# A recurrent-memory transformer layer: a new order of TensorE work, wider last-row projection, kept weights, no padding loads

## The chip, the cores and the metric

The kernel runs on one core of a Trainium2 chip. The metric is device time in microseconds (us), from one launch to its end; lower is better. "PE" is TensorE (its matmuls), "PEld" its weight loads, "DVE" VectorE, "ACT" ScalarE, "POOL" GpSimd and "SP" SyncE, whose queue issues the DMAs.

## The reference, cut to what matters

```python
# x (1, 2048, 512), mem0 (1, 8, 512), 32 heads of 128, seg_len 32, bf16
h  = x + A(layernorm(x))
h2 = h + B(layernorm(h))

def A(x):
    mem = mem0
    for s in range(64):
        xs = x[:, 32 * s:32 * s + 32]
        hcat = concat([mem, xs])                # 8 memory rows + 32 token rows
        q, k, v = (einsum('btd,dhe->bhte', hcat, W) for W in (Wq, Wk, Wv))
        scores = einsum('bhqe,bhke->bhqk', q, k) * 128 ** -0.5
        scores = where(mask, scores, -1e9)      # memory seen by all; tokens causal
        o = einsum('bhqk,bhke->bhqe', softmax(scores), v)
        o = einsum('bhte,hed->btd', o, Wo)
        mem = o[:, :8]                          # feeds the next segment
        outs.append(o[:, 8:])
    return concat(outs)

def B(x):                                       # MLP, inner width 1792
    return einsum('bsf,fd->bsd', gelu(einsum('bsd,df->bsf', x, w1) + b1), w2) + b2
```

The memory rows that a segment puts out are the memory rows that the next one takes in, so the 64 segments run one after the other. The MLP is free of that chain.

## The kernel before, in words

**Rows.** A segment has 8 memory rows and 32 token rows. The kernel works on packs of 32 rows: pack A of a segment holds its first 24 token rows (`NA`) and the 8 memory rows. The last 8 token rows of four segments make pack B of a block of 128 tokens (`hB`, `KB`, `QTB`, `VSB`, `VBD`, `OTB`). Pack B depends on no memory, so its Q, K and V are computed a block ahead. `bk = s // 4` is the block of segment `s` and `sg = s % 4` its place in it.

**Work of one segment on PE.** Each name below is a stage in the tuple `ORDER`, which fixes by hand the order of PE's work in a segment, in units (stage, from unit, to unit).

- `Q0 K0 Q1 K1 V0 V1`: projections of pack A, half of the heads each. A pass (`passes`, L670) is four units, one for each 128 of the contraction of 512; a unit is four matmuls 512 wide on the four 32-column tiles of the array, each with its weight load of 128x32 (`hT`). ACT casts the result out of PSUM into `kq` (L688, L689), DVE transposes it (L711) into `KALL` and `QT`; `ZC` (L725, L732) takes the memory and last-row queries.
- `SC0 SC1` (`sc_mm`, L815): scores of the memory rows and last rows, 16 heads each; then `sc_softmax`: maximum `nmc`, exponential `EC`, reciprocal `rsc`, product `PC`, transpose `PTC` (L824 to L835). A score bank is filled with the mask ahead of the matmuls (`prefill`).
- `SA` (`sa_mm`, L874): scores of the 24 token rows, and the softmax into `PTA`.
- `PV0 PV1` (`pv_c`, L846 and L850): value products of memory and last rows, with the array tiled by rows; copies to `OT` and `OTB`.
- `PVA` (`pv_a`, L903): value products of the token rows of the segment before, also tiled by rows; `pv_a_ev` copies them to `OT`.
- `WO` (`wo`, `wo_units`, L931): output projection, 64 matmuls 256 wide in 8 units; its 32 rows are this segment's memory rows and the token rows of an earlier segment. DVE transposes the result (`TT`, L943) and adds its two halves (L937): the memory columns of the next segment's `hT`, and the token rows into `opT`.
- `F0 F1`: in `sg` 0, 1 and 2 the K, Q and V passes of the next block's pack B; in `sg` 3 the output projection of pack B of the block before (`wo_B`), in eight units that take the place of the passes.

**Out of the recurrence.** `nat` brings `opT` by a DMA transpose into `oN`, adds it to the residual `xr` (L967), takes the statistics for the second layer norm and writes `h_mid`. It runs two blocks behind. The MLP runs at the end, in four superblocks of 512 tokens (L1260, L1267, L1313); some of its loads and first matmuls lie in the last segments.

**Order on the other engines.** `Sched` records every operation with what it reads and writes. PE's order is as written; DVE, ACT, POOL and SP get theirs from list scheduling with estimated durations, in which `BONUS` shifts priorities by kind. An operation with alternatives (`either`) goes to ACT or DVE. `BANK` says which PSUM bank each stage uses: 0 to 3 are `quad`, 4 to 7 `ps`.

**Alignment.** `align` counts PE instructions and, with `PHASE` set, puts up to eight padding weight loads into a pass (L668) until every segment starts at a chosen count modulo 256. With `KEEP` set, the passes run through the contraction forth and back (`directions`), and a unit whose weights are those already loaded is issued as `matmul_kept`, without loads.

The order of one segment before:

```python
ORDER = (("PVA", 0, 99), ("Q0", 0, 4), ("K0", 0, 4), ("Q1", 0, 4), ("K1", 0, 4), ("SC0", 0, 99), ("V0", 0, 4),
         ("V1", 0, 2), ("SC1", 0, 99), ("SA", 0, 99), ("V1", 2, 4), ("F0", 0, 2), ("PV0", 0, 99), ("F0", 2, 4),
         ("PV1", 0, 99), ("WO", 0, 8), ("F1", 0, 4))
```

Of the kernel before, what the change touches and what calls it, by code (L numbers as in the profile page):

```python
# [27 lines left out]
BONUS = {"EC0": 9.64, "EC1": 2.52, "KA1": 1.19, "KB0": -4.21, "KB1": 40, "OTB": -3, "OTm0": 25.44, "OTm1": -8.14, "OTx": 40, "PA": -3.16, "PC0": 2.46, "PC1":  # L28
# [3 lines left out]
         4.71, "kq1": 12.67, "kq2": 10.08, "kq5": 6.67, "maskA": -7.3, "maskAF": -11.82, "maskCF": -12.78, "maskL": 40, "maskR": 2.12, "nma": -4.99,  # L32
         "nmc0": 40, "nmc1": 40, "oN": -40, "opA": 4.9, "opB": -1.91, "rs": 40, "rs2": -8.34, "rsa": -1.22, "rsc0": -3.89, "rsc1": -3.1, "sma": -4.13,
         "st2": -40, "vd": -1.71, "xT": 0.29, "xn": -10, "xr": 3.08}
LEAN = 0.36
# [13 lines left out]
class Op:  # L49
    __slots__ = ("eng", "fn", "reads", "writes", "idx", "gidx", "deps", "sig", "sigcount", "waits",  # L50
                 "tag", "pad", "held", "name", "is_dma", "dma_sem", "dur", "mode", "rank", "start", "succ", "prev", "ni", "dma_count", "alts", "kind")

    def __init__(self, eng, fn, reads, writes, name, dur, mode):
        self.eng, self.fn, self.reads, self.writes = eng, fn, reads, writes
        self.name, self.dur, self.mode = name, dur, mode
        self.deps, self.waits, self.succ = [], [], []
        self.tag = self.pad = self.held = None
        self.sig = self.is_dma = False
        self.sigcount = 0
        self.dma_sem = None  # L60
        self.rank = self.start = 0.0
        self.idx = -1
        self.prev = None
        self.alts = None
        k = writes[0] if writes else ""
        self.kind = k if isinstance(k, str) else k[0] + (str(k[-1]) if k[0] in HALVES else "")


class Sched:
# [181 lines left out]
    def finalize(self):  # L251
# [5 lines left out]
        for o in self.all_ops:  # L257
            E = o.eng
            cand, dwaits = {}, []
            for p in o.deps:  # L260
                if p.is_dma:
                    if p not in dma_known[E]:
                        dwaits.append(p)
                    continue
                if p.eng == E and E not in self.self_sync:
                    continue
                if p.idx > cand.get(p.eng, -1):
                    cand[p.eng] = p.idx
            waits = []
            for F, i in cand.items():  # L270
# [107 lines left out]
P = 128  # L378
# [62 lines left out]
def build_kernel(nc, A_x, A_mem0, A_Wq, A_Wk, A_Wv, A_Wo, B_w1, B_b1, B_w2, B_b2, out):  # L441
# [3 lines left out]
    with st:  # L445
# [47 lines left out]
        TT = sb("TT", [P, 2, DC, 2, 32], F32)  # L493
        TTB = sb("TTB", [P, DC, 2, 32], F32)
        opT = sb("opT", [P, 2, DC, P])
# [342 lines left out]
        def pv_c(s, r):  # L838
            par, bk, sg = s % 2, s // 4, s % 4

            def f(e):
                for i in range(4):
                    for j in range(4):
                        rows = slice(32 * j, 32 * j + 32)
                        c0 = 16 * (i % 2)
                        e.matmul(quad[:, j, (4 * r + i) * 16:(4 * r + i) * 16 + 16], VS[rows, s % 3, r, i * E:(i + 1) * E], PTC[rows, r, c0:c0 + 16, i // 2],  # L846
                                 start=(i == 0), stop=False, tile_position=(32 * j, 0), skip_group_check=True)
                for j in range(4):
# [16 lines left out]
        def sa_mm(s, bank):  # L865
            par = s % 2

            prefill("maskAF", maskAF, 256, ps[bank][:, 0:256], ("ps", bank))

            def f(e):  # L870
                for k in range(8):
                    for j in range(4):
                        h = 16 * (k // 4) + 4 * j + k % 4
                        ins = e.matmul(ps[bank][32 * j:32 * j + 32, 32 * k:32 * k + 32], QT[:, h // 2, :, h % 2], KALL[:, par * HP + h // 2, :, h % 2], start=False, stop=(k == 7),  # L874
                                       tile_position=(0, 32 * j), skip_group_check=True)
                return ins
            S.op("pe", f, reads=[("QT", 0), ("QT", 1), ("KA", par, 0), ("KA", par, 1)], writes=[("ps", bank)], dur=0.25, mode=MC, ni=64)
            v = ps[bank][:, 0:256].rearrange("p (a t) -> p a t", a=8)

# [16 lines left out]
        def pv_a(s):  # L896
            par = s % 3

            def f(e):
                for k in range(8):  # L900
                    for j in range(4):
                        rows = slice(32 * j, 32 * j + 32)
                        ins = e.matmul(quad[:, j, 256 + 24 * k:280 + 24 * k], VS[rows, par, k // 4, (k % 4) * E:(k % 4 + 1) * E], PTA[rows, s % 2, k // 2, 0:NA, k % 2],  # L903
                                       start=(s == NS - 1 and k == 0), stop=True, tile_position=(32 * j, 0), skip_group_check=True)
                return ins
            S.op("pe", f, reads=[("VS", par, 0), ("VS", par, 1), ("PTA", s % 2)], writes=QK, dur=0.26, mode=MR, ni=64)

        def pv_a_ev(s):
            opar = s % 2
            src = quad[:, :, 256:448].rearrange("p j (k q) -> p j k q", k=8)  # L910
            ot = OT[:, opar, :, 0:NA].rearrange("p (j k) q -> p j k q", k=8)
# [42 lines left out]
        def wo_B(bk, bank):  # L954
            wo_units(lambda sl: OTB[:, bk % 2, sl, :], lambda r: [("OTB", bk % 2, sg) for sg in range(4)], bank)
            S.op("dve", lambda e: e.transpose(TTB[:].rearrange("p c q t -> p (c q t)"), ps[bank][:, 0:256]), reads=[("ps", bank)], writes=["TTB"], dur=t_dve(256) + 0.02)
            t5 = TTB[:].rearrange("p c q (s t) -> p c q s t", s=4)
            o = opT[:, bk % 2, :, :].rearrange("p c (s t) -> p c s t", s=4)[:, :, :, NA:SEG]
            S.op("dve", lambda e: [e.tensor_tensor(o[64 * q2:64 * q2 + 64], t5[0:64, :, q2], t5[64:128, :, q2], ALU.add) for q2 in range(2)][1],
                 reads=["TTB"], writes=[("opB", bk % 2)], dur=0.6)  # L960

        def nat(bk):

            S.dma(lambda e: e.dma_start_transpose(oN[:], opT[:, bk % 2].rearrange("p c t -> p (c t)")), 256,
                  reads=[("opA", bk % 2, k) for k in range(4)] + [("opB", bk % 2)], writes=["oN"])
            xs = xr[:, bk % XR, :]
            S.op("dve", lambda e: e.tensor_tensor(xs, xs, oN[:].rearrange("p c t -> p (c t)"), ALU.add), reads=["oN", ("xr", bk % XR)], writes=[("xr", bk % XR)], dur=0.43)  # L967
            i = bk % 2
# [122 lines left out]
        for s in range(NS):  # L1091
# [46 lines left out]
            def after_pv1(f):  # L1138
                if "PV1" in done or not any(n[:2] == "SC" for n in done):
                    f()  # L1140
# [5 lines left out]
            def part(name):  # L1146
# [46 lines left out]
                elif name == "SA":  # L1193
                    sa_mm(s, bank_of[name])
                elif name == "PVA":
                    if s > 0:
# [9 lines left out]
            if s == 0:  # L1206

                for n in START:
# [15 lines left out]
                    elif n == "X":  # L1224
                        ln1(1)
                    elif n == "Z":
                        qb_fill(0)
# [53 lines left out]
        for i in range(2):  # L1281
# [3 lines left out]
        p2_T(1)  # L1285

        rest = [lambda: wo(NS, 6, mem=False), lambda: pv_a(NS - 1), lambda: pv_a_ev(NS - 1), lambda: nat(NTB - 2), lambda: wo(NS + 1, 7, mem=False),
                lambda: wo_B(NTB - 1, 6), lambda: None, lambda: nat(NTB - 1)]
# [83 lines left out]
```

## Time and profile before

| | |
|---|---|
| runs | 861.02 us median of 3 (857.36 to 864.41) |
| profiled execution | span 869.8 us |
| PE | 92% busy, 22,121 matmuls |
| PEld | 57% busy, 24,182 weight loads |
| DVE | 66%, 1,870 instructions |
| ACT | 64%, 1,547 instructions |
| POOL | 10%, 205 instructions |
| mean granted clock | 0.986 |
| segments 1 to 62 | 57.00 to 750.66 us |
| before and after them | 57.00 us and 119.14 us |

The profiled execution is 8.8 us longer than the median of the runs. Its first 57 us are the loading of the weights and segment 0. Then follow 62 segments of the same shape, and at the end the last segment and the MLP. Nearly all the time lies in the 62 segments, so the thing to read is one segment, instruction by instruction. In a timeline, a group's length runs to the end of its last instruction while the next group has already begun; the time it takes from PE is the distance to the next group's start.

### The profile page before, as it was taken

The page shows a single profiled execution, that of the slowest core. Times are in us where ns is not written, and L with a number is a line of the kernel's source. Part 1 is how long each engine was busy: PE and PEld are TensorE (multiplying, and loading weights), DVE is VectorE, ACT ScalarE, POOL GpSimd, SP SyncE. Part 2 cuts the span into 40 slices and gives each one's busy share as a digit, 9 for nine tenths or more (in the row PEclk, how much of TensorE's full clock was granted, in tenths as well). Part 3 has the DMA queues.
Part 4 walks back from the last instruction along what each step waited for, and adds up shares of the span by engine and source line. Part 5 has one row for each costly group of instructions (what it writes and reads, how often), then busy time and mean ns, then how long its engine had stood idle before and what let it go on. Part 6 is the DMA issues. An engine that isn't in the chain of part 4 may idle for free.

```text
span 869.8 us, 50658 instructions
## 1 busy us (share of the span) xinstructions
PE 800.3 (92%) x22121; PEld 492.4 (57%) x24182; DVE 576.8 (66%) x1870; ACT 555.6 (64%) x1547; POOL 87.5 (10%) x205
## 2 busy tenths in 40 slices
PE   3588999999999999999999998999999999889998
PEld 1245666666656666666656665665656665544443
DVE  3267677878787878787878786867687867534111
ACT  2347676767676767676767776767676758922332
POOL 4021000101010101010010101000000000006200
PEclk9879999999999999999999999999999999999999
DMA  9951000110101010101010101010113120254100
GB/s 357 366 163 22 5 26 19 28 30 25 31 23 34 23 35 19 32 20 37 16 40 16 41 17 40 11 34 11 34 28 65 46 77 16 87 171 112 49 24 25
DMA packets 65937, 49.01 MB, mean 56 GB/s; under 512 B 28468, under 2 KB 62140, under 8 KB 65724
## 3 DMA queue, kind: packets, MB, share of 16 engines
q1 hardware_dynamic: 65392, 45.50, 18.0%
q8 instruction: 182, 2.98, 1.5%
q14 instruction: 31, 0.25, 0.1%
q10 hardware_dynamic: 332, 0.27, 0.1%
HBM read 31.34 MB, written 8.39 MB: 46 GB/s over the span
## 4 chain that ended last, share of the span: by engine, by line
PE 85%; DVE 6%; issue 4%; DMA 3%; ACT 2%; SPq 0%; ACTq 0%; DVEq 0%
PE ps L670 45%; PE ps L931 19%; PE quad L1267 6%; PE ps L1260 4%; PE quad L846 4%; PE quad L903 2%; PE quad L815 2%; PE ps L1069 2%; DVE PC L834 1%; DMA WQ<-in_A_Wq_dram 1%; DVE nma L884 1%; DVE nmc L824 1%; DMA xr<-in_A_x_dram 1%; PE ps L874 1%; PE quad L850 1%
## 5 line engine op out<-in xcount | busy, mean ns | idle before, releaser
L670 PE MATMUL ps<-WQ,hT 128*32 128x512 bf16 x2048 | 140.2, 382 | 3.3 <-DVE hT L937 2.3
L670 PE MATMUL ps<-WK,hT 128*32 128x512 bf16 x2048 | 137.9, 379 | 0.3 <-issue 0.3
L670 PE MATMUL ps<-WV,hT 128*32 128x512 bf16 x2032 | 136.1, 381 | 0.0
L931 PE MATMUL ps<-WO,OT 128*32 128x256 bf16 x4224 | 130.6, 277 | 0.0
L689 ACT ACTIVATE kq<-ps 128x512 bf16<-128x512 f32 x160 | 94.8, 593 | 51.8 <-PE ps L670 50.6
L688 ACT CAST OT<-quad 128x128 bf16<-128x128 f32 (+1 forms) x147 | 73.1, 497 | 81.0 <-PE quad L903 56.4
L688 ACT CAST kq<-ps 128x512 bf16<-128x512 f32 x160 | 93.4, 583 | 34.6 <-PE ps L670 34.5
L931 PEld LDWEIGHTS ps<-WO,OT 128*32 128x32 bf16 x4224 | 108.4, 98 | 7.6 <-issue 1.7
L711 DVE STREAM_TRANSPOSE QT<-kq 128x256 f32<-128x256 f32 x128 | 57.0, 446 | 65.3 <-ACT kq L689 65.0
L670 PEld LDWEIGHTS ps<-WK,hT 128*32 128x32 bf16 x2048 | 64.0, 97 | 39.9
L828 ACT ACTIVATE EC<-quad,nmc 128x64 f32<-128x64 f32 x252 | 77.1, 311 | 13.0 <-DVE nmc L824 12.9
L711 DVE STREAM_TRANSPOSE KALL<-kq 128x256 f32<-128x256 f32 x160 | 71.3, 446 | 18.2 <-ACT kq L688 10.2
L670 PEld LDWEIGHTS ps<-WQ,hT 128*32 128x32 bf16 x2048 | 57.6, 95 | 31.0 <-issue 5.3
L688 ACT CAST VS<-ps 128x512 bf16<-128x512 f32 x127 | 74.1, 584 | 0.0
L732 POOL COPY ZC<-QTB 128x256 bf16<-128x256 bf16 x64 | 25.7, 402 | 430.8 <-PE quad L815 401.4
L670 PEld LDWEIGHTS ps<-WV,hT 128*32 128x32 bf16 x2032 | 54.6, 96 | 21.9 <-issue 1.8
L846 PEld LDWEIGHTS quad<-PTC,VS 32*128 32x128 bf16 x2048 | 25.8, 91 | 66.2 <-ACT OT L688 24.6
L931 PE MATMUL ps<-WO,OTB 128*32 128x256 bf16 x1024 | 42.7, 276 | 21.8 <-issue 21.7
L1263 ACT ACTIVATE WQ<-ps,b1t 128x512 bf16<-128x512 f32 x42 | 28.9, 688 | 51.9 <-PE ps L1260 51.9
L846 PE MATMUL quad<-PTC,VS 32*128 32x16 bf16 x2048 | 38.6, 168 | 15.8 <-DVE rsc L831 5.8
L1313 DVE TENSOR_TENSOR WV<-quad,WV 128x512 bf16<-128x512 f32 x16 | 11.1, 692 | 60.7 <-PE quad L1267 60.7
L815 PEld LDWEIGHTS quad<-KALL,ZC 128*32 128x32 bf16 x2016 | 36.5, 96 | 25.5 <-DVE KALL L711 14.2
(143 smaller groups left out, 1297.9 us busy)
## 6 DMA issues: line engine op xcount, KB each, us to landing
WV<-in_A_Wv_dram SPq DMA_DIRECT2D x4, 1024.0 KB, 9.1
WK<-in_A_Wk_dram SPq DMA_DIRECT2D x4, 1024.0 KB, 16.8
v_last<-VSB SPq DMA_DIRECT2D x64, 64.0 KB, 2.1
WQ<-in_A_Wq_dram SPq DMA_DIRECT2D x4, 1024.0 KB, 8.5
VBD<-v_last SPq DMA_DIRECT2D x64, 64.0 KB, 2.1
WO<-in_A_Wo_dram SPq DMA_DIRECT2D x4, 1024.0 KB, 13.3
WK<-in_B_w_dram SPq DMA_DIRECT2D x4, 896.0 KB, 7.5
h_mid<-xr SPq DMA_DIRECT2D x16, 128.0 KB, 1.8
```

The lines of the kernel that those rows point to most:

```text
L670: ins = e.matmul(o, l, m, start=(k == 0), stop=(k == DC - 1), tile_position=(0, 32 * j), skip_group_check=True)
L688: return {"act": (lambda e: e.copy(out, src), t_act(n, ps_)), "dve": (lambda e: e.tensor_copy(out, src), 0.16 + 1.042e-3 * n * fast)}
L689: return {"act": (lambda e: e.mul(out, src, scale_), t_act(n, ps_)), "dve": (lambda e: e.tensor_scalar(out, src, scale_, None, ALU.mult), ...
L711: S.op("dve", lambda e: e.transpose(out, src), reads=[("kq", i)], writes=[key], dur=t_dve(256) + 0.02)
L732: S.op("pool", lambda e: e.tensor_copy(dst, src), reads=[("QTB", bk % 2, q) for q in range(2)], writes=[("ZCb", par)], dur=0.45)
L815: ins = e.matmul(o[32 * j:32 * j + 32, 64 * sl:64 * sl + 64], ZC[:, par, h, :], rhs, start=False, stop=(i == 3), tile_position=(0, 32 * j) ...
L828: ins = e.activation(EC[:, r, sl, :], o[:, 64 * sl:64 * sl + 64], ACTF.Exp, bias=nmc[:, r, sl:sl + 1], accum_out=smc[:, r, sl:sl + 1])
L846: e.matmul(quad[:, j, (4 * r + i) * 16:(4 * r + i) * 16 + 16], VS[rows, s % 3, r, i * E:(i + 1) * E], PTC[rows, r, c0:c0 + 16, i // 2], st ...
L931: ins = e.matmul(ps[bank][32 * j:32 * j + 32, 0:256], lhs(slot(h)), wo_cols(h, b), start=(k == 0), stop=(k == 15), tile_position=(0, 32 * ...
L1260: ins = e.matmul(ps[bank][:, 0:SBT], W1[:, cc, fc * P:(fc + 1) * P], hnT_of(k)[:, cc, :], start=(cc == 0), stop=(cc == DC - 1))
L1263: S.op("act", lambda e: e.activation(gT[:, fc, :], ps[bank][:, 0:SBT], ACTF.Gelu_apprx_tanh, bias=b1t[:, fc:fc + 1], scale=1.0), reads=[(" ...
L1267: S.op("pe", lambda e: e.matmul(quad[:, t, :], gT_of(k, fc)[:, t * P:(t + 1) * P], W2[:, fc, :], start=(fc == 0), stop=(fc == FC - 1)), re ...
```

## The change

- `ORDER`: PVA moves from the head of the segment to right before PV0; SC0 goes between the halves of K1; WO is cut into two halves, one between F0's first half and PV1, one after F0's second half; SA goes to the end.
- `BANK` and `BONUS` are new; the evacuation of PVA (`pv_a_ev`) is placed after PV1.
- `PHASE` is empty: no padding loads. `KEEP` is on: adjacent passes of one pack share the loaded weights where they meet.
- `wo_B` is 32 matmuls 512 wide in eight units instead of 64 of 256; its four partial sums of 32 rows are added by an ACT copy and two DVE adds into `oBn`, in natural layout. `Op.alone` makes the next DVE operation wait for the last of them.
- `nat` brings these rows into `oN` by four small DMAs after its transpose and before the add to `xr`; `opT` is cleared on POOL at the start.
- `pv_a` writes 32 columns per head instead of 24, each with the start flag set.
- `SA` could also use a bank of `quad`, and a stage `SAP` exists in the code; neither is used by the order.

```diff
-PHASE = (87, 24, 172, 102)
-KEEP = False
+PHASE = ()
+KEEP = True
...
-ORDER = (("PVA", 0, 99), ("Q0", 0, 4), ("K0", 0, 4), ("Q1", 0, 4), ("K1", 0, 4), ("SC0", 0, 99), ("V0", 0, 4), ("V1", 0, 2), ("SC1", 0, 99), ("SA", 0, 99),
-         ("V1", 2, 4), ("F0", 0, 2), ("PV0", 0, 99), ("F0", 2, 4), ("PV1", 0, 99), ("WO", 0, 8), ("F1", 0, 4))
-BANK = dict(K0=7, K1=5, Q0=6, Q1=4, V0=6, V1=4, F0=6, F1=7, FB=5, SC0=0, SC1=1, SA=7, WO=4)
+ORDER = (("Q0", 0, 4), ("K0", 0, 4), ("Q1", 0, 4), ("K1", 0, 2), ("SC0", 0, 99), ("K1", 2, 4), ("V0", 0, 4), ("V1", 0, 2), ("SC1", 0, 99),
+         ("V1", 2, 4), ("PVA", 0, 99), ("PV0", 0, 99), ("F0", 0, 2), ("WO", 0, 4), ("PV1", 0, 99), ("F0", 2, 4), ("WO", 4, 8), ("F1", 0, 4),
+         ("SA", 0, 99))
+BANK = dict(K0=7, K1=4, Q0=6, Q1=5, V0=5, V1=6, F0=4, F1=5, FB=5, SC0=0, SC1=7, SA=4, WO=6)
...
+            if o.idx > 0 and self.streams[E][o.idx - 1].alone:
+                cand[E] = o.idx - 1
...
+        S.op("pool", lambda e: e.memset(opT[:], 0.0), writes=["opT0"] + [("opA", i, k) for i in range(2) for k in range(4)], dur=1.0)
...
-                        e.matmul(quad[...], VS[...], PTA[rows, s % 2, k // 2, 0:NA, k % 2], start=(s == NS - 1 and k == 0), ...)
+                        e.matmul(quad[...], VS[...], PTA[rows, s % 2, k // 2, :, k % 2], start=(k == 0), ...)
...
         def wo_B(bk, bank):
-            wo_units(lambda sl: OTB[:, bk % 2, sl, :], lambda r: [("OTB", bk % 2, sg) for sg in range(4)], bank)
-            S.op("dve", ... transpose TTB <- ps[bank][:, 0:256] ...)
-            S.op("dve", ... two halves_add of TTB into opT ..., writes=[("opB", bk % 2)])
+            for k in range(8):
+                def f(e, k=k):
+                    for j in range(4):
+                        h = 8 * j + k
+                        ins = e.matmul(ps[bank][32 * j:32 * j + 32, :], OTB[:, bk % 2, slot(h), :], WO[:, h, :], start=(k == 0), stop=(k == 7),
+                                       tile_position=(0, 32 * j), skip_group_check=True)
+                    return ins
+                S.op("pe", f, ..., mode=MC, ni=8)
+            part_sum = view(OTB, (bk % 2) * H * 32, [64, D], F32)
+            S.op("act", lambda e: e.copy(part_sum, ps[bank][64:128, :]), ...)
+            S.op("dve", lambda e: e.tensor_tensor(part_sum, ps[bank][0:64, :], part_sum, ALU.add), ...)
+            S.op("dve", lambda e: e.tensor_tensor(oBn[:], part_sum[0:32], part_sum[32:64], ALU.add), ...).alone = True
 
         def nat(bk):
             S.dma(lambda e: e.dma_start_transpose(oN[:], opT[:, bk % 2].rearrange("p c t -> p (c t)")), 256, ...)
+            rows = oN[:].rearrange("p c t -> p (c t)")
+            for sg in range(4):
+                S.dma(lambda e, sg=sg: e.dma_start(rows[32 * sg + NA:32 * sg + SEG, :], oBn[8 * sg:8 * sg + 8, :]), 8, reads=["oBn", "oN"], writes=[("oNr", sg)])
             S.op("dve", lambda e: e.tensor_tensor(xs, xs, oN[:].rearrange("p c t -> p (c t)"), ALU.add),
-                 reads=["oN", ("xr", bk % XR)], ...)
+                 reads=["oN", ("xr", bk % XR)] + [("oNr", k) for k in range(4)], ...)
```

The kernel's PE instructions fall from 46,617 (22,121 matmuls, 24,182 weight loads of which 2,077 are padding, the rest semaphore waits) to 42,232 (21,605 matmuls, 1,276 of them without a load).

More of the change, by code (lines that the diff above doesn't have):

```diff
@@ L866, in sa_mm @@
             par = s % 2
-            prefill("maskAF", maskAF, 256, ps[bank][:, 0:256], ("ps", bank))
+            o = quad[:, bank, 256:512] if bank < 4 else ps[bank][:, 0:256]
+            prefill("maskAF", maskAF, 256, o, ("ps", bank))
             def f(e):
@@ L902, in f @@
                         rows = slice(32 * j, 32 * j + 32)
-                        ins = e.matmul(quad[:, j, 256 + 24 * k:280 + 24 * k], VS[rows, par, k // 4, (k % 4) * E:(k % 4 + 1) * E], PTA[rows, s % 2, k // 2, 0:NA, k % 2],
-                                       start=(s == NS - 1 and k == 0), stop=True, tile_position=(32 * j, 0), skip_group_check=True)
+                        ins = e.matmul(quad[:, j, 256 + 32 * k:288 + 32 * k], VS[rows, par, k // 4, (k % 4) * E:(k % 4 + 1) * E], PTA[rows, s % 2, k // 2, :, k % 2],
+                                       start=(k == 0), stop=True, tile_position=(32 * j, 0), skip_group_check=True)
                 return ins
@@ L954, in wo_B @@
         def wo_B(bk, bank):
-            wo_units(lambda sl: OTB[:, bk % 2, sl, :], lambda r: [("OTB", bk % 2, sg) for sg in range(4)], bank)
[L956 to L960, printed above, removed]
+            for k in range(8):
[5 more added lines that the diff above has]
+                    return ins
+                S.op("pe", f, reads=[("WO", g) for g in range(4)] + [("OTB", bk % 2, sg) for sg in range(4)], writes=[("ps", bank)], dur=0.216, mode=MC, ni=8)
@@ new lines, in wo_B @@
+            okeys = [("OTB", bk % 2, sg) for sg in range(4)]
+            part_sum = view(OTB, (bk % 2) * H * 32, [64, D], F32)
+            S.op("act", lambda e: e.copy(part_sum, ps[bank][64:128, :]), reads=[("ps", bank)], writes=okeys, dur=t_act(512))
+            S.op("dve", lambda e: e.tensor_tensor(part_sum, ps[bank][0:64, :], part_sum, ALU.add), reads=[("ps", bank)] + okeys, writes=okeys, dur=t_dve(512))
+            S.op("dve", lambda e: e.tensor_tensor(oBn[:], part_sum[0:32], part_sum[32:64], ALU.add), reads=okeys, writes=["oBn"], dur=t_dve(512)).alone = True
@@ L1138, in after_pv1 @@
             def after_pv1(f):
-                if "PV1" in done or not any(n[:2] == "SC" for n in done):
+                if "PV1" in done:
                     f()
@@ L1225, in build_kernel @@
                         ln1(1)
+                    elif n == "SA" and any(k == "SAP" for k, _, _ in ORDER):
+                        pass
                     elif n == "Z":
```

31 lines of the change are left out of this document (18 added, 13 removed), and 8 rows, old and new, of the table BONUS.

## The prediction

> **What bounds the kernel now.** I read the page first, then the windows of the recurrence (columns: span; busy time and records of PE, PEld, DVE, ACT, POOL; clock; DMA share; GB/s), then PE's timeline with its gaps, then one whole segment.
>
> ```profile
> span 869.8 us, 50658 instructions
> PE 85%; DVE 6%; issue 4%; DMA 3%; ACT 2%; SPq 0%; ACTq 0%; DVEq 0%
> L931 PE MATMUL ps<-WO,OTB 128*32 128x256 bf16 x1024 | 42.7, 276 | 21.8 <-issue 21.7
> q8 instruction: 182, 2.98, 1.5%
> ...
> 57.00:750.66 693.66, 657.44 (x20625) 425.36 (x22625) 527.37 (x1759) 492.61 (x1430) 56.87 (x144) 1.00 0.12 29
> 300.10:312.18 12.08, 10.70 (x368) 7.37 (x407) 8.50 (x29) 7.46 (x23) 1.94 (x5) 1.00 0.26 60
> 312.18:323.12 10.94, 10.58 (x334) 6.51 (x364) 8.55 (x29) 8.20 (x24) 0.40 (x1) 1.00 0.07 15
> 323.12:333.86 10.74, 10.55 (x335) 6.60 (x373) 8.47 (x30) 7.82 (x24) 0.40 (x1) 1.00 0.06 17
> 333.86:344.54 10.68, 10.56 (x340) 7.12 (x337) 9.08 (x31) 8.02 (x24) 1.19 (x3) 1.00 0.06 17
> 750.66:869.80 119.14, 110.75 (x982) 53.11 (x1061) 31.22 (x70) 45.17 (x76) 19.71 (x20) 0.98 0.29 85
> ```
>
> PE sets the time: 85% of the chain is PE work, and in a segment DVE and ACT leave 2 to 4 us free. Segments 1 to 62 take 693.66 us, 44.75 per four; the four shown take 44.44. I call one such four a block: the change is worked out per block and multiplied by 62/4 = 15.5. The segment that also projects the last rows (wo_B, the first shown) takes 12.08 against 10.68 to 10.94, and that line alone has 21.7 us of PE idle put down to issue. PE's timeline, and the DMA window 308.3 to 309.6, say what the idle is:
>
> ```profile
> 307.58 1.93 PE L931 MATMUL ps<-WO,OT 128*32 128x256 bf16 x64
> 309.34 0.28 PE L931 MATMUL ps<-WO,OTB 128*32 128x256 bf16 x3
> 310.88 1.03 PE L931 MATMUL ps<-WO,OTB 128*32 128x256 bf16 x29 [1.26 <-issue]
> ...
> 765.34 1.03 PE L931 MATMUL ps<-WO,OTB 128*32 128x256 bf16 x29 [4.02 <-issue]
> ...
> q8 instruction: 1, 0.02, 5.9%
> ```
>
> PE stops after three matmuls of wo_B, for 1.26 us, while q8 moves one packet of 16 KB. 182 packets serve about 46,600 PE instructions, one per 256: PE has run out of instructions. Here is a whole segment:
>
> ```profile
> 322.54 0.62 PE L903 MATMUL quad<-PTA,VS 32*128 32x24 bf16 x32
> 323.12 1.06 PE L670 MATMUL ps<-WQ,hT 128*32 128x512 bf16 x16
> 325.70 0.45 DVE L711 STREAM_TRANSPOSE KALL<-kq 128x256 f32<-128x256 f32 x1 [0.16 <-ACT kq L688]
> 326.59 0.31 PE L815 MATMUL quad<-KALL,ZC 128*32 128x64 bf16 x16
> 326.71 1.48 PE L670 MATMUL ps<-WV,hT 128*32 128x512 bf16 x24
> 326.81 0.59 ACT L688 CAST kq<-ps 128x512 bf16<-128x512 f32 x1
> 327.18 0.22 DVE L725 COPY ZC<-QT 128x128 bf16<-128x128 bf16 x1
> 327.43 0.45 DVE L711 STREAM_TRANSPOSE KALL<-kq 128x256 f32<-128x256 f32 x1
> 328.00 0.32 PE L815 MATMUL quad<-KALL,ZC 128*32 128x64 bf16 x16
> 328.12 0.43 PE L874 MATMUL ps<-KALL,QT 128*32 128x32 bf16 x32
> 328.39 0.63 PE L670 MATMUL ps<-WV,hT 128*32 128x512 bf16 x8
> 329.64 0.27 PE L846 MATMUL quad<-PTC,VS 32*128 32x16 bf16 x16 [0.19 <-DVE rsc L831]
> 329.88 0.61 PE L670 MATMUL ps<-WQ,hB 128*32 128x512 bf16 x8
> 330.01 0.27 ACT L688 CAST OT<-quad 128x128 bf16<-128x128 f32 x1
> 330.42 0.43 PE L846 MATMUL quad<-PTC,VS 32*128 32x16 bf16 x16
> 330.83 1.93 PE L931 MATMUL ps<-WO,OT 128*32 128x256 bf16 x64
> 332.59 1.04 PE L670 MATMUL ps<-WQ,hB 128*32 128x512 bf16 x16
> 332.82 0.45 DVE L943 STREAM_TRANSPOSE TT<-ps 128x256 f32<-128x256 f32 x1 [0.18 <-PE ps L931]
> 333.30 0.39 DVE L937 TENSOR_TENSOR hT<-TT 64x32 bf16<-64x32 f32 x2
> 333.56 0.37 PE L903 MATMUL quad<-PTA,VS 32*128 32x24 bf16 x32
> 333.86 1.21 PE L670 MATMUL ps<-WQ,hT 128*32 128x512 bf16 x16
> ```
>
> Lengths on PE are differences of starts. Q0, K0, Q1 and K1 are 16 groups of four matmuls from 323.12 to 326.59: 0.217 a group. A score product takes 0.12, SA 0.27, WO 1.76. Entering the row-tiled mode costs 0.10 (332.59 + 4 x 0.217 = 333.46, PVA at 333.56), PVA 0.30, PV0 or PV1 0.24. Of the 0.24, 20 matmuls at PVA's pace of about 0.005 make 0.10, leaving the mode 0.14. Work of a segment: 32 groups 6.94 + scores 0.24 + SA 0.27 + two PV 0.68 + WO 1.76 + PVA 0.40 = 10.29. The rest of the 10.74 is PV0 late by 0.28 (free at 328.39 + 0.87 + 0.10 = 329.36) and 0.17 at PV1 (0.41 where PV0 took 0.24). Four times 10.57 is 42.28; wo_B and the other gaps hold 2.16 of the 44.44 beyond F's work, part of it in PVA (0.58 at 322.54, not 0.30).
>
> **The change part by part.** Loads dropped: the built order has 2,077 padding loads fewer, 512 go with wo_B and about 1,260 matmuls reuse weights; it falls to 42,232 instructions, 165 fetches. In the windows, 373 loads against 337 make a segment 0.06 longer, which its 0.17 gap covers. Direct price: 0, up to a gain of 0.06 / 36 x 3,849 = 6.4 us.
>
> wo_B: 64 matmuls of 256 become 32 of 512, 8 groups, 1.73, what F takes in the other segments. So 12.08 loses its 1.26, and the other gaps go where no block of instructions is consumed faster than one arrives. The block that ended at the stop held PV0, half of wo_B's first units, PV1, WO and three matmuls, about 3 us; the densest of the segment at 323.12 takes some 3.4 and cost 0.17. In the new order the boundaries fall at 2.5 per segment: from V0 to the first unit of WO, or from the end of PVA to F1, 3.5 to 3.8 us by the same lengths. Taken: no gap; bound 0.17 in four blocks of instructions per four segments, 0.68.
>
> Token value products moved next to PV0: one entry and one exit fewer, -0.24 per segment; 32 columns instead of 24 add 0 to 0.05, I take 0. Work: 10.05.
>
> Waits in the new order. Group counts are PE's way; the chain is KALL, softmax or copy:
> - SC0 now stands after 14 groups (3.04), its KALL ended at 326.15 and 0.12 of hand-over follows (327.88 to 328.00): 3.15. Wait 0.11.
> - SC1: K1's last group now ends behind SC0, near 3.70; ACT starts 0.22 later (326.59 to 326.81), 0.59, KALL 0.45, 0.12: 5.08 against 5.00. A ZC copy of 0.22 may stand before it: 0.1 to 0.3, I take 0.20.
> - PV0: SC0 to PV0 took 3.05, so 6.20; PE is there at 5.20 + SC1 0.12 + two groups 0.43 + entry 0.10 + PVA 0.16 = 6.01. That is 0.19, and up to 0.64 where one DVE pass of SA's softmax, 0.45 like TT, slips into the chain; most of SA's passes lie earlier, so I take 0.24.
> - WO, first half: OT's copy at 330.01 ends 0.64 after PV0's start, 0.14 hand-over, 0.78, against 0.24 + 0.43 of cover: 0.11. Second half behind PV1 the same: 0.11.
> - Q0: from the end of WO 1.10 (332.59 to 333.30 + 0.39) and a hand-over that I put at 0.09, between nothing and KALL's 0.12: 1.19 against F1 and SA, 1.13: 0.06.
>
> Sum 0.83, where 0.28 stood. SA's softmax moves beneath the next Q and K passes, whose DVE has over a microsecond free; without it, each 0.45 pass would delay KALL and so SC0. The OT evacuation behind PV1 is needed only two segments later. What queues behind each of these waits is PE's whole order, so each counts in full.
>
> After wo_B, ACT copies 64x512 and DVE adds twice, in the place of one transpose and two adds:
>
> ```profile
> L1313 DVE TENSOR_TENSOR WV<-quad,WV 128x512 bf16<-128x512 f32 x16 | 11.1, 692 | 60.7 <-PE quad L1267 60.7
> L959 DVE TENSOR_TENSOR opT<-TTB 64x128 bf16<-64x128 f32 x32 | 9.2, 289 | 0.7
> v_last<-VSB SPq DMA_DIRECT2D x64, 64.0 KB, 2.1
> ```
>
> DVE: 2 x 0.69 against 0.45 + 2 x 0.29: +0.35, bounds 0 (free time) and 0.35; with the KALL chains of the next segment right behind, I take 0.30. The four small DMAs per block stand on SP ahead of the next transfers, land in about 2.1 like the rows shown, and their add is read two blocks after the projection: 0; if the cover goes, about 2 us per block on DVE. The clearing of opT on POOL stands at the very start, beneath the first weight transfers: 0; POOL is nearly idle (56.87 of 693.66), so 1 us of it delays nothing else.
>
> Sum per block: 4 x (10.05 + 0.83) + 0.30 = 43.82, so -0.62 against 44.44, x 15.5 = -9.6. Tail (119.14): +1.1, because the MLP's first bank is now held by SA until two DVE passes of 0.45 and their hand-overs; -1.6 of the 4.02 gap (bounds 0 and -4.0), the half that fewer instructions spare. Together -10.1. The profiled execution, 869.8, lies 8.8 over the median of the runs, 861.02; I carry the difference over: **851**.
>
> **The rivals.** *Late chains (slower):* the group of 16 that starts at 333.86 shows 1.21 where 323.12 shows 1.06: in such segments the last column tiles end 0.15 late, and the passes hand that on. Then SC0, SC1 and PV0 each wait 0.15 more: sum of waits 1.28. In all segments +27.9, 879; in half, 865. It decides from a sum of 0.98 per segment. For: the old order had slack at SC0 and SC1, the new one has none. Against: seen in one segment of the four.
>
> *Fetch gaps come back elsewhere (slower):* one 1.26 gap per block stays: +1.26 x 15.5 = 19.5, 871; with 0.17 at four places 861.5. For: two dense stretches per segment now. Against: q8 moved 16 KB while PE stood, and fewer blocks are asked for. The Trainium skill ("Runtime: NRT & Kernel Launch", "Instruction fetch mechanics") has the sequencer stream blocks of 256 instructions with the crossing mostly hidden; by that rule the gap is no fetch and stays, which is this rival; the trace, with 1.26 us beside a q8 packet, disagrees.
>
> *Gain eaten (same):* waits of 0.95 to 1.0 per segment (0.12 to 0.17 more, x 62): 858 to 861. *More gain:* SC1's wait of 0.20 gone (ACT and DVE free just then), 0.20 x 62 = 12.4: 839.
>
> **How the numbers follow.** Forecast 0.50 (845 to 857, a third of it above 852.4), more gain 0.15, gain eaten 0.13, late chains 0.13, fetch gaps 0.09. One per cent, 8.6 us, is about what a measurement can tell from no change: faster 0.33 + 0.15 = 0.48, same 0.17 + 0.13 = 0.30, slower 0.22. Range 839 to 870: from the gain with small waits to the half case of late chains and the one-gap case.
>
> **What would show it.** Right: Q0 to Q0 near 10.9 (11.2 behind a wo_B), the wo_B segment within 0.4 of the others, 165 packets on q8, under 5 us of issue before wo_B, PV0 waiting on PTC and SC0 on KALL by the amounts above. Wrong: Q0 to Q0 above 11.1, gaps of 0.4 or more at other places of 256 instructions, or SC0, SC1 and PV0 waiting over 0.25 each.

## The result, and the profile after

The changed kernel takes 869.63 us (median of 4 runs, 866.56 to 873.29) against 860.74 us before on the same chip: ratio 1.0108, interval 1.0067 to 1.0148. A second measurement on another chip gave 881.21 against 867.58, ratio 1.0142 (1.0104 to 1.0180). It is 1.1 to 1.4% slower, clear of the noise both times; the forecast was 1.2% faster. The chips differ by nearly 1%, so below ratios are compared, or traces of kernels that ran beside nearly the same time of before (866 to 869 us).

First the page after (its profiled execution took 868.58 us with a span of 866.9), with the lines that answer to those of before:

```profile
span 866.9 us, 46398 instructions
PE 805.1 (93%) x21587; PEld 402.5 (46%) x20329; DVE 583.4 (67%) x1848; ACT 546.8 (63%) x1570; POOL 88.3 (10%) x206
...
q8 instruction: 165, 2.70, 1.2%
...
PE 81%; DMA 5%; DVE 5%; ACT 4%; issue 3%; POOL 1%; SPq 1%; ACTq 0%; DVEq 0%
...
L938 PE MATMUL ps<-WO,OT 128*32 128x256 bf16 x4224 | 143.7, 275 | 9.7 <-issue 7.0
```

Everything that was to be saved is saved: 165 fetches instead of 182, loads down by a sixth, and of the 21.8 us of idle at wo_B's own matmuls only a stop of 3.4 in the tail is left. But WO, which had no idle before, now shows 9.7 us. The windows (columns as before: length, then busy time and records of each engine, clock, DMA share, GB/s), first segments 1 to 62, then four segments beginning with the one that holds wo_B, then the tail:

```profile
56.14:746.30 690.16, 663.94 (x20173) 338.70 (x18943) 529.05 (x1729) 483.22 (x1450) 58.95 (x144) 1.00 0.13 30
301.27:312.81 11.54, 10.95 (x342) 5.65 (x310) 7.37 (x25) 7.72 (x25) 1.20 (x3) 1.00 0.22 56
312.81:323.81 11.00, 10.75 (x340) 5.43 (x311) 9.50 (x30) 7.78 (x24) 1.30 (x3) 1.00 0.06 19
323.81:334.49 10.68, 10.68 (x344) 5.45 (x313) 8.84 (x29) 7.96 (x25) 1.18 (x3) 1.00 0.05 15
334.49:345.15 10.66, 10.66 (x342) 5.39 (x312) 8.85 (x29) 7.68 (x24) 0.42 (x1) 1.00 0.08 19
746.30:866.90 120.60, 109.91 (x933) 50.16 (x916) 34.82 (x76) 46.51 (x79) 19.84 (x20) 0.99 0.29 83
```

These four take 43.88 where the sum said 43.82, so over four segments the forecast looks right. Two things do not fit. The first segment of the four still holds 0.88 more than the two clean ones (11.54 against 10.66). And the tail is longer than before, not shorter. PE's timeline in that first segment shows where the 0.88 is:

```profile
304.07 0.40 PE L676 MATMUL ps<-WK,hT 128*32 128x512 bf16 x4
304.44 0.30 PE L821 MATMUL quad<-KALL,ZC 128*32 128x64 bf16 x16
...
306.08 0.39 PE L676 MATMUL ps<-WV,hT 128*32 128x512 bf16 x4
306.43 0.30 PE L821 MATMUL ps<-KALL,ZC 128*32 128x64 bf16 x16
...
307.10 0.37 PE L910 MATMUL quad<-PTA,VS 32*128 32x32 bf16 x32
307.44 0.27 PE L852 MATMUL quad<-PTC,VS 32*128 32x16 bf16 x16
...
308.22 1.05 PE L938 MATMUL ps<-WO,OT 128*32 128x256 bf16 x30
309.86 0.28 PE L938 MATMUL ps<-WO,OT 128*32 128x256 bf16 x2 [0.59 <-issue]
```

The small waits stand where they were foretold: SC0 begins 0.37 after the last group of K1's first half, of which 0.22 is that group (0.15 wait, 0.11 foretold); SC1 0.35 after its group (0.13, 0.20 foretold). But PE stops for 0.59 us two matmuls before the end of WO's first half, and that is again an empty instruction queue, in another place.

The profiled execution of the first chip is no fair partner to the one of before, so the loss is placed by two traces taken beside like times: before unchanged (866.8 us with a span of 865.0) and after unchanged (span 881.8). The windows of each are segments 1 to 7, 8 to 55, 56 to 62, and the tail; first before, then after:

```profile
57.27:134.16 76.89, 69.80 (x2241) 46.23 (x2647) 56.40 (x188) 53.04 (x159) 10.16 (x26) 1.00 0.09 20
134.16:666.63 532.47, 511.20 (x16135) 330.18 (x17458) 412.39 (x1375) 377.71 (x1104) 42.63 (x108) 1.00 0.11 28
666.63:746.65 80.02, 74.01 (x2261) 46.20 (x2557) 58.36 (x198) 62.62 (x167) 3.99 (x10) 1.00 0.16 43
746.65:865.00 118.35, 109.16 (x965) 53.07 (x1037) 30.99 (x70) 45.09 (x76) 19.74 (x20) 0.99 0.30 85
```
```profile
55.12:136.36 81.24, 71.96 (x2204) 37.20 (x2065) 57.04 (x183) 50.40 (x158) 10.22 (x26) 0.98 0.10 22
136.36:679.47 543.11, 521.08 (x15757) 265.13 (x14788) 412.39 (x1352) 373.93 (x1129) 44.60 (x108) 1.00 0.12 28
679.47:760.93 81.46, 76.52 (x2225) 38.53 (x2085) 59.72 (x195) 59.36 (x164) 4.20 (x10) 1.00 0.16 42
760.93:881.80 120.87, 111.30 (x970) 50.40 (x932) 34.89 (x76) 46.80 (x79) 19.76 (x20) 0.99 0.30 83
```

Of the 16.8 us between these two spans, 10.6 are in the steady segments (45.26 per four against 44.37), 4.4 in segments 1 to 7, 1.4 in 56 to 62, 2.5 in the tail, and -2.1 before segment 1. The clock column of segments 1 to 7 reads 0.98 in the trace of after and 1.00 in that of before, so a part of the 4.4 (some 1.6 us at most, an estimate from 2% of 81.24) is the clock and not the change.

### The profile page after: what moved, and what is told of

It reads as the page before. It is cut to its first block, busy times and chain, and to the rows that moved or that the text cites. A ratio compares the mean times of both kernels' runs of the same rounds, so it can differ in the third digit from the quotient of the medians.

```text
span 866.9 us, 46398 instructions
## 1 busy us (share of the span) xinstructions
PE 805.1 (93%) x21587; PEld 402.5 (46%) x20329; DVE 583.4 (67%) x1848; ACT 546.8 (63%) x1570; POOL 88.3 (10%) x206
## 4 chain that ended last, share of the span: by engine, by line
PE 81%; DMA 5%; DVE 5%; ACT 4%; issue 3%; POOL 1%; SPq 1%; ACTq 0%; DVEq 0%
PE ps L676 37%; PE ps L938 14%; PE ps L428 7%; PE quad L1290 4%; PE ps L1283 4%; PE ps L967 3%; PE quad L852 3%; PE quad L821 2%; PE ps L881 2%; PE quad L910 2%; PE ps L821 2%; DMA WQ<-in_A_Wq_dram 1%; ACT kq L694 1%; POOL WV L1045 1%; DMA v_last<-VSB 1%
## 5 line engine op out<-in xcount | busy, mean ns | idle before, releaser
L676 PE MATMUL ps<-WQ,hT 128*32 128x512 bf16 x1796 | 120.1, 381 | 4.2 <-DVE hT L944 4.2
L676 PE MATMUL ps<-WV,hT 128*32 128x512 bf16 x1528 | 118.4, 380 | 0.0
L676 PE MATMUL ps<-WK,hT 128*32 128x512 bf16 x1544 | 118.1, 381 | 0.0
L950 DVE STREAM_TRANSPOSE TT<-ps 128x256 f32<-128x256 f32 x66 | 29.7, 450 | 86.8 <-PE ps L938 86.8
L676 PEld LDWEIGHTS ps<-WQ,hT 128*32 128x32 bf16 x1796 | 43.6, 96 | 52.6 <-issue 21.6
L717 DVE STREAM_TRANSPOSE QT<-kq 128x256 f32<-128x256 f32 x128 | 56.9, 445 | 14.7 <-ACT kq L695 10.6
L676 PEld LDWEIGHTS ps<-WV,hT 128*32 128x32 bf16 x1528 | 40.1, 97 | 52.9 <-issue 40.8
L676 PEld LDWEIGHTS ps<-WK,hT 128*32 128x32 bf16 x1544 | 38.5, 97 | 55.3 <-issue 41.7
L428 PE MATMUL ps<-WV,hT 128*32 128x512 bf16 x520 | 52.4, 380 | 0.0
L1338 DVE TENSOR_TENSOR WV<-quad,WV 128x512 bf16<-128x512 f32 x16 | 11.1, 692 | 60.0 <-PE quad L1290 52.4
L834 ACT ACTIVATE EC<-ps,nmc 128x64 f32<-128x64 f32 x130 | 39.6, 309 | 15.8 <-DVE nmc L830 15.6
L428 PE MATMUL ps<-WK,hT 128*32 128x512 bf16 x504 | 49.5, 379 | 0.0
L694 DVE CAST VS<-ps 128x512 bf16<-128x512 f32 x64 | 43.7, 683 | 5.0 <-PE ps L428 5.0
L676 PE MATMUL ps<-WK,hB 128*32 128x512 bf16 x512 | 38.3, 390 | 6.7 <-ACT VSB L694 5.7
```

The source lines that it names most:

```text
L428: return e.add_instruction(mybir.InstMatmult(name="I-%d" % (4000000 + _kept[0]), engine=mybir.EngineType.PE, start_tensor_calc=start, stop ...
L676: ins = e.matmul(o, l, m, start=(k == 0), stop=(k == DC - 1), tile_position=(0, 32 * j), skip_group_check=True)
L694: return {"act": (lambda e: e.copy(out, src), t_act(n, ps_)), "dve": (lambda e: e.tensor_copy(out, src), 0.16 + 1.042e-3 * n * fast)}
L717: S.op("dve", lambda e: e.transpose(out, src), reads=[("kq", i)], writes=[key], dur=t_dve(256) + 0.02)
L834: ins = e.activation(EC[:, r, sl, :], o[:, 64 * sl:64 * sl + 64], ACTF.Exp, bias=nmc[:, r, sl:sl + 1], accum_out=smc[:, r, sl:sl + 1])
L950: S.op("dve", lambda e: e.transpose(tt.rearrange("p c q t -> p (c q t)"), ps[bank][:, 0:256]), reads=[("ps", bank)], writes=[("TT", par)], ...
```

## The experiments

### Before again, and after again

Both unchanged. They give the traces just read.

> The kernel before, unchanged, for a second trace. Supply theory (the profiled execution of before, 871.5 us with what lies around its span, was a slow one, 10 us over the median, and what was slow in it is the supply of PE with instructions): this execution is near 861, PE's idle put down to issue before L931 is 10 to 17 us instead of 21.7, and the segments without such a gap keep their 10.53 to 10.73. Order theory (the profiled execution of before was an ordinary one, and the new order lost its gain in dependency waits): the trace shows again about 21 us of issue before L931, a wo_B segment of about 12 us, and the time is still 861 with a span near 870.

Measured: 865.63 against 865.76, ratio 0.9991 (0.9971 to 1.0012). L931's idle put down to issue in the wo_B line is 19.0 us, not 21.7, and that segment still takes 11.9 on average over segments 8 to 55. So the first trace of before was only a few us slow; supply stalls of this size are ordinary, and the supply theory's 10 to 17 us was wrong. The order theory was right on the stalls, but not on the span: it is 865.0 and not near 870.

> After, unchanged, against before on the same chip. Ends theory (in segments 8 to 55 after is about even with before, 44.2 to 44.4 per four; the loss lies in segments 1 to 7, 56 to 62 and the tail): ratio 1.008 to 1.014, with segments 1 to 7 longer by 2 to 4 us than in the second trace of before, 56 to 62 by 0.5 to 3.5, the tail by 2 to 4.5. Body theory (the steady segments lose): per four segments over 44.8.

Measured: ratio 1.0142 (1.0104 to 1.0180). The steady segments take 45.26 per four: the body theory's bound is passed. The ends are there too (4.4, 1.4 and 2.5, each within or near what was foretold, with the reservation on the clock made above). Both theories held half.

### Before with only the padding left out

```diff
-PHASE = (87, 24, 172, 102)
+PHASE = ()
```

> Before, with only the padding loads left out. If padding loads cost time of their own (up to 33 us is PEld's busy time with them), 845 to 855. If they only hold the 256-instruction boundaries in harmless places, the boundaries drift, gaps appear in other segments, and the time is the same or longer: 861 to 875. My expectation is the second.

Measured: 854.78 against 865.76, ratio 0.9864 (0.9813 to 0.9915), 174 fetches. My expectation, the same time or longer, was the wrong one. The line of wo_B in before (second trace) and in this kernel:

```profile
L931 PE MATMUL ps<-WO,OTB 128*32 128x256 bf16 x1024 | 43.2, 278 | 19.0 <-issue 19.0
```
```profile
L931 PE MATMUL ps<-WO,OTB 128*32 128x256 bf16 x1024 | 38.0, 273 | 4.2 <-issue 4.2
```

The same 1,024 matmuls lose 15 us of idle without being touched (the second line is from an execution of 849.13 us, under the median of 854.78). The stop in wo_B was no property of its width: the alignment put a 256-instruction boundary there in every block of four segments. The stops do not all go: other lines now hold stops of up to 1.7 us, and over the whole kernel PE's idle put down to issue falls from 22 to 13 us.

### Before with the wide wo_B alone, and without padding

wo_B, its sums and nat as in after; ORDER, BANK, BONUS and KEEP as before.

> Before, with only wo_B changed: 32 matmuls of 512, the ACT copy, the two DVE adds and the four small DMAs. Supply theory: the gap in the middle of wo_B goes (1.0 us in each of 15 blocks of four segments in an ordinary execution), and so does most of the 4.02 in the tail: 843 to 852. Rival (the DVE adds and the DMAs after wo_B take back what the projection gains): 856 to 866, with the segment after wo_B 0.3 to 0.6 longer.

Measured: 878.66 against 865.76, ratio 1.0149 (1.0108 to 1.0189). The wo_B segment fell from 11.9 to 11.0, but the one behind it rose from 11.1 to 13.1. Its PE timeline, and the group of padding loads here and in before:

```profile
317.54 0.40 PE L673 MATMUL ps<-WK,hT 128*32 128x512 bf16 x4
318.64 0.83 PE L673 MATMUL ps<-WK,hT 128*32 128x512 bf16 x12 [0.69 <-issue]
320.44 0.31 PE L818 MATMUL quad<-KALL,ZC 128*32 128x64 bf16 x16 [0.97 <-ACT ZC L728]
...
L671 PEld LDWEIGHTS <-hT 128*32 128x32 bf16 x2959 | 47.8, 96 | 21.8 <-DVE hT L940 1.7 <-issue 1.6
```
```profile
L668 PEld LDWEIGHTS <-hT 128*32 128x32 bf16 x2077 | 33.1, 96 | 14.9 <-DVE hT L937 1.7 <-issue 1.6
```

Of the 1,024 instructions that wo_B saved, 882 were put back as padding by the alignment (2,959 padding loads, 181 fetches), now in the next segment's Q and K passes, where the new stop of 0.69 stands. And SC0 waits 0.97 for ZC.

> Before, with the wide wo_B and without padding loads, order as before. Supply theory (PE is paced by blocks of 256 instructions; padding loads cost blocks, and in the wide version they were bunched into the next segment's Q and K passes, which made the 13 us loss): 8 blocks fewer from the padding and 4 more from the width, ratio to before 0.970 to 0.988. Rival (the sums and small DMAs after the wide projection cost by themselves, as the 0.97 wait on ZC suggests): 0.995 to 1.010.

Measured: 864.82 against 866.34, ratio 0.9974 (0.9953 to 0.9995): the rival's range. Against the padding-free kernel with the narrow wo_B the wide projection costs 1.1%. The stops of 0.69 are gone, the wait on ZC stays, once per block:

```profile
313.91 0.30 PE L818 MATMUL quad<-KALL,ZC 128*32 128x64 bf16 x16 [1.05 <-ACT ZC L728]
```

### The wide wo_B with its sums elsewhere in the queues

```diff
-"OTB": -3,
+"OTB": 10,
```

On top of the kernel above: a higher priority for the ACT copy and the DVE add behind wo_B. The kind `OTB` also holds the copies that bring the last rows out of PV0 and PV1, so these move too; the run does not tell the two apart.

> Before, with the wide wo_B, no padding, and one priority changed (OTB from -3 to 10), which puts ACT's and DVE's sums of wo_B elsewhere in their queues. If the 1.06 wait on ZC in the first segment of each block is a matter of that order and nothing else is wrong with the wide projection: the wait goes, per four segments 42.8 to 43.4, ratio 0.970 to 0.988, at or below the kernel without padding alone (0.986). If the sums cost by their length: ratio 0.993 to 1.000.

Measured: 848.52 against 867.58, ratio 0.9770 (0.9726 to 0.9813). The 14 waits of SC0 on ZC, 14.9 us in all, are gone, per four segments 43.56, a little over the 43.4 foretold. So the length of the sums cost little; the place of these operations in ACT's and DVE's queues cost 1 us per block. This version is 2.3% under before.

### Kept weights, and what is left for the order

```diff
-KEEP = False
+KEEP = True
```

> The same without kept weights, for the comparison on the same chip: 0.973 to 0.982.

> Before's order with the wide wo_B, no padding, OTB at 10, and now also kept weights: all of after's parts but the new order, its banks and priorities, and the 32 columns. If kept weights are worth nothing (in the new order their removal left the ratio at 1.015): 0.973 to 0.982, and the new order is then what costs after its 3.8 per cent. If kept weights pay in the old order because they save blocks of instructions there: 0.955 to 0.970.

Measured beside each other: 0.9797 (0.9756 to 0.9838) without and 0.9806 (0.9775 to 0.9837) with kept weights. The kept weights show no gain, in 166 fetches against 170. The kernel with kept weights holds every part of the change but the order with its banks and priorities, the 32 columns and the later evacuation of PVA; its `OTB` at 10 is not in the change. Its windows, in the same four stretches:

```profile
57.56:132.62 75.06, 68.75 (x2209) 38.15 (x2097) 56.56 (x189) 53.40 (x160) 10.13 (x26) 1.00 0.13 21
132.62:652.31 519.69, 505.94 (x15755) 279.60 (x14977) 416.63 (x1374) 379.64 (x1105) 43.31 (x108) 1.00 0.13 29
652.31:732.02 79.71, 75.17 (x2236) 40.04 (x2112) 58.76 (x197) 62.83 (x167) 3.97 (x10) 1.00 0.19 43
732.02:848.10 116.08, 109.30 (x924) 50.19 (x896) 31.61 (x69) 46.55 (x78) 20.25 (x20) 1.00 0.32 86
```

Against after (span 881.8): 23.4 us in the steady segments, 6.2 in the first seven, 1.8 in 56 to 62, 4.8 in the tail. With 1.0142 against 0.9806, what is left of the change, the new order and what goes with it, costs 3.4%, and takes back more than the 2% that the rest gains.

In the steady segments the stops are only about half of it. Two segments of this kernel in which PE does not stop at a boundary, from Q0 to Q0:

```profile
294.46:304.96 10.50, 10.38 (x330) 5.72 (x314) 8.09 (x28) 7.52 (x24) 1.19 (x3) 1.00 0.28 69
316.04:326.60 10.56, 10.37 (x334) 5.70 (x312) 8.44 (x29) 7.77 (x24) 0.40 (x1) 1.00 0.06 17
```

The first holds wo_B; the segment behind it takes 10.57 at best. Four of them without a stop make about 42.1. In after the clean segments take 10.66 to 10.68, and 11.00 behind wo_B, which makes 43.0. So of the 1.95 us per four segments between the two kernels (45.26 against 43.31) about 0.9 lies in segments where PE does not stop, and 1.0 or so in stops. This is an estimate from single segments of two traces.

> After, with every matmul of the passes loading its own weights again (about 1,260 loads more, 170 blocks instead of 165). If loads themselves cost nothing and only blocks count: 5 blocks more and boundaries that drift through the segment, ratio to before 1.010 to 1.030. If reusing weights was itself a cost (a kept matmul that has to wait for its group): below 1.005.

Measured, after without kept weights: ratio 1.0150 (1.0109 to 1.0190) with 170 fetches, and after itself 1.0142: no difference from the other side either. Five blocks more did not show.

### After with the old wo_B, and with the old order

> After, with wo_B, its sums and nat as before (64 matmuls of 256, no small DMAs). Supply theory: the block of instructions from V0 to WO in the wo_B segment has 64 more instructions in the same time, its gap grows from 0.6 to more than 1 us, and a second one may come: 875 to 890. Rival (the sums and DMAs after the wide wo_B are what costs): 860 to 868.

Measured: 901.75 against 865.76, ratio 1.0441 (1.0382 to 1.0500), 46.4 per four segments. In the new order the 256-wide wo_B costs 3% more than the wide one; the supply theory's direction was right, its size too small.

> After, with ORDER, BANK and BONUS of before: wide wo_B, kept weights, no padding, 32 columns, but the old order. If the new order itself is what loses: ratio to before 0.965 to 0.985, clearly under after's 1.011. If the order is neutral and the sums after wo_B or the kept weights lose: 1.000 to 1.015.

Measured: 891.96 against 866.34, ratio 1.0300 (1.0262 to 1.0339). It settles nothing on the order. This kernel does not compute the layer: its output is off by orders of magnitude, and why is not known. And in the old order PVA stands at the head of the segment, where it now waits for ACT's copies into `OT` (25.9 us in 15 waits, up to 2.2), most likely because its evacuation was placed behind PV1. The kernel with kept weights above, which leaves PVA and its evacuation as before, is the fair one.

### Where the stop in after comes from

Three kernels on after: the VBD loads issued behind the last WO unit of the fourth segment; no v_last and VBD transfers at all from block 2 on; and a shift of all boundaries by half a block of instructions. The edits:

```diff
 def v_B_in(bk, after=()):            # late: called in sg 3, after = [last WO unit]
...
 def v_B_spread(bk):                  # none
+    if bk >= 2:
+        return
...
-                owed = (PHASE[seg % 4] - at) % FETCH_N
+                owed = 128 if seg == 4 else 0        # shift
```

> After, with the four VBD loads of each block issued behind the last WO unit of the fourth segment instead of in its V passes. Supply theory (in the fourth segment the fetch that PE needs in WO starts about 2 us after its boundary instead of 0.5, because the VBD loads lie ahead of it in the DMA engines): the gap before the last WO matmuls, 0.6 to 1.2 us, goes, 44.2 per four segments becomes 43.4 or less, ratio to before 0.993 to 1.002. Rival (the gap belongs to the density of instructions there): ratio as after's, 1.007 to 1.015.

Measured: 1.0149 (1.0097 to 1.0201), 44.5 per four segments. The stop stays, and in nine of the twelve blocks of segments 8 to 55 the packet still starts 2.0 to 2.5 us after the boundary in V0.

> After, without the v_last and VBD transfers from block 2 on (the last rows' values are then those of blocks 0 and 1). If these transfers are what makes the fetch late in the fourth segment: its gap of 0.6 to 1.2 us goes, per four segments 43.0 to 43.6, ratio 0.985 to 0.998. If not: 1.005 to 1.015, with the fetch starting again 1.5 to 2.5 us after the boundary in V0.

Measured: 1.0093 (1.0062 to 1.0123), 44.9 per four segments. The stop shrinks to 0.39 (median of the blocks) but does not go, and the packet still starts 1.5 us or more after the boundary in V0 (median 1.8), with the DMA engines all but idle until then. These transfers make it worse; they are not its cause. The kernel leaves out the transfers that renew the last rows' values, and its profiled execution took 880.5 us against a median of 875.2.

> After, with 128 extra weight loads once, in segment 4, so that all later boundaries of 256 instructions fall half a block away: in the fourth segment of a block they are then in K0, at the end of PVA and in F1 instead of in V0 and WO. Position theory (a gap needs a boundary ahead of a dense stretch at the time when the fourth segment's transfers run): the gap before WO goes, per four segments 43.0 to 43.7, ratio 0.988 to 1.000. Rival (the gap belongs to the number of blocks or to the fourth segment's work): 1.007 to 1.015.

Measured: 1.0186 (1.0127 to 1.0246), 45.5 per four. The fourth segment's WO loses its stop, and others come: its wo_B now holds eight, of up to 0.89, and the second segment of each block, clean before the shift, takes 11.7. The position decides where PE stops, not whether.

What a stop consists of shows in the second trace of after. PE's timeline, then what the DMA view says of the windows 349.15 to 350.2 and 358.8 to 360.3 (queue, packets, MB, share of 16 engines), then the stretch between two boundaries as windows, the first without a stop, the second with one:

```profile
346.59 0.37 PE L910 MATMUL quad<-PTA,VS 32*128 32x32 bf16 x32
...
351.55 1.04 PE L676 MATMUL ps<-WV,hB 128*32 128x512 bf16 x14 [0.91 <-issue]
...
361.84 0.29 PE L938 MATMUL ps<-WO,OT 128*32 128x256 bf16 x2 [1.17 <-issue]
...
q8 instruction: 1, 0.02, 5.6%
...
q8 instruction: 1, 0.02, 5.8%
...
341.62:346.76 5.14, 5.14 (x143) 1.91 (x123) 4.48 (x17) 4.18 (x13) 0.00 (x0) 1.00 0.01 3
346.76:351.55 4.79, 3.88 (x155) 2.42 (x139) 3.74 (x13) 2.74 (x9) 0.42 (x1) 1.00 0.16 31
```

From its first instruction to its last each stretch holds 256 instructions of PE, counted by their starts (the counts in the view are higher, because they take in those that began earlier and still ran). The one through the Q, K and V passes keeps PE busy for 5.14 us; the one from PVA through both halves of WO for 3.88. By the packet's times in the trace, the next block's packet starts 2.4 us after the boundary at 346.76, takes 1.0, and PE goes on 1.4 after it has landed: 4.8 from boundary to boundary. Behind 5.14 us of work that would be hidden; where PE has 3.88, it stops. The stretch that holds the 1.17 runs the same way: the packet starts 2.2 us after the boundary at 356.64 in V0, takes 1.4, and PE goes on 1.6 after it. In three later blocks of the same trace the packet starts 0.5 to 0.6 us after that boundary, and the stretch takes 3.7 us; in the nine others it starts 1.9 to 2.6 after, and the stretch takes 4.4 to 5.2. So the stop goes with the late packet. The Trainium skill ("Runtime: NRT & Kernel Launch", "Instruction fetch mechanics") calls the crossing of a 256-instruction boundary mostly hidden; here stops of 0.59, 0.91 and 1.17 us stand at such boundaries, so in a stream this dense it is not.

## Why the prediction was wrong, point by point

- **The sum's mechanism for the order held.** Clean segments take 10.66 to 10.68: work of 10.05 and waits of 0.62 instead of 0.83. The segment behind wo_B takes 0.33 more, 0.30 foretold. Without stops four segments would take 4 x 10.67 + 0.33 = 43.0, below the 43.82. That the four shown take 43.88 is luck: the waits were 0.8 us shorter than summed, and stops made up for it. Nor is 43.0 a gain of the order, and the sum had not made it one: 10.88 stood there for a segment against 10.57 before, so that all of the forecast gain had to come from stops that go.
- **"Taken: no gap" failed**, and with it the forecast. Measured are 44.22 per four over segments 8 to 55 on the first chip and 45.26 on the second: 1.2 to 2.3 of stops. I had taken the 3.5 to 3.8 us of a block as enough because 3.4 had cost 0.17; only PE's work in a block was weighed, not when its packet starts. The supply of a block took 4.8 us in the case above. The first trace of before had it too: counted back 256 instructions, the block that ended at the 1.26 stop began at 306.04, not some 3 but 3.6 us before PE stopped, its packet started 2.3 us later and took 1.2, and PE went on after 4.84. The rival "fetch gaps come back elsewhere", with 1.26 per block and 871 us, is what happened; I gave it 0.09. Gaps of 0.4 us or more at other boundaries were named as the sign of being wrong, and they came.
- **The gain of wo_B was put down to its width.** Most of the 21.7 us were the padding's doing: 19.0 became 4.2 without padding. Left for the width, once its sums stand well, is 0.7 to 0.9% (0.9797 and 0.9770 against 0.9864), about as much as these measurements can tell.
- **The direct price of padding** was bounded by "0, up to a gain of 6.4"; leaving the padding out gained 11 us, and the idle put down to issue fell by 9. For the kept weights 0 was right.
- **The tail and the ends.** The sum had -0.5 for the tail, taken from 1.1 and -1.6; measured are +1.5 between the two first traces and +2.5 between the two second ones. PE's timeline of the tail in the first trace after:

```profile
760.50 0.83 PE L967 MATMUL ps<-WO,OTB 128*32 128x512 bf16 x12 [3.36 <-issue]
761.16 0.42 PE L881 MATMUL ps<-KALL,QT 128*32 128x32 bf16 x32
763.09 1.49 PE L1088 MATMUL ps<-hnT,QTB 128*128 128x512 bf16 x3 [1.51 <-DVE SA L892]
```

  SA's hold on the bank costs 1.51 where 1.1 stood, and the tail's stop is 3.36, not 2.4. Segments 1 to 7 (+4.4, a part of it clock) and 56 to 62 (+1.4) were not in the sum at all: it multiplied one steady block by 15.5. In segment 2 of the first trace, SC0 alone waits 1.22 for KALL, whose DVE queue stands behind a norm that waits for a DMA:

```profile
69.13 0.41 DVE L619 TENSOR_SCALAR xn<-xr,agg,rst 128x512 bf16<-128x512 bf16 x1 [1.27 <-DMA xT<-xn]
...
71.42 0.30 PE L821 MATMUL quad<-KALL,ZC 128*32 128x64 bf16 x16 [1.22 <-DVE KALL L717]
```

- **Late chains** did not come: the waits at SC0, SC1 and PV0 stayed under 0.2 in the steady segments shown.

What stays open: in the second trace of after the same boundary in V0 is followed by its packet after 0.4 to 1.4 us in the second segment of a block (median 0.65) and after up to 2.6 in the fourth (median 2.15). Neither moving nor leaving out the VBD transfers did away with that. That the new order stops more than the old one with as many blocks (165 against 166), because its dense stages lie together from PVA to WO, is argued from block lengths; the order's moves were not tried one by one, and which of them makes the clean segments 0.1 to 0.4 us longer than in the old order is not shown either.

## What to carry to other kernels

When an engine waits on "issue", look at how many instructions lie between two boundaries of 256 and how long the engine has work for them, before crediting the stop to the line where it appears: a neighbour's padding, or none, can move it. In this kernel fewer instructions gained nothing where they were dropped from the passes, which are sparse already. And a saving on one engine is only worth it if the operations that replace it on the others stand in a good place of their queues; one priority was worth 1 us per block here.

## What the runs showed of the hardware that was not expected

Dropping some 1,260 weight loads between matmuls of 512 columns gained nothing that these runs could tell: 0.9797 without kept weights against 0.9806 with them, and 1.0150 against 1.0142. Leaving out 2,077 padding loads gained 1.4%, with 9 us less of PE's idle put down to issue. From one 256-instruction boundary to the next PE took 4.8 us in the case above with 3.9 us of work, of which the packet itself was 1.0; the rest lay before its start and between its landing and PE's next matmul.
